# VectorE's order written out in the tiles of seven products: the fifth product's addition, S3's subtraction and S4's split

## The chip, the cores and the metric

The kernel runs on one core of one Trainium2 chip. The metric is the device time of one execution in microseconds (us); lower is better. A core has five engines that run their own instruction streams and wait for each other through semaphores: TensorE (PE in the profile, with its weight loads as PEld), VectorE (DVE), ScalarE (ACT), GpSimd (POOL) and SyncE (SP, which issues DMAs here).

## The reference

An attention layer is followed by two feed-forward layers. The change lies in the second of these (`_moe2_ref`), whose first half computes a gate and a value from the same input and multiplies them:

```python
def _moe2_ref(x, w_gate, w_val, w_out):       # x is 896 x 768, w_gate and w_val 768 x 1536
    g = x @ w_gate
    silu = g * (1.0 / (1.0 + np.exp(-g)))
    val = x @ w_val
    return (silu * val @ w_out).astype(np.float32)
```

All inputs arrive as float64 or float32 and the matmuls run on pairs of rounded float32 numbers: each operand is split into a high part (a rounding copy) and a low part (what the copy left out), and a product is high x high + high x low + low x high.

## The kernel before

The 1536 gate and value columns are worked off in 12 tiles `fc` of 128 columns. Tiles 1 to 6 (`ff2_gv_seven`) do not compute gate and value apart. They take the 128 gate columns and the 128 value columns of the tile as the rows of a 2 x 2 block matrix, whose columns are the two halves of the 768 inputs, and multiply it with the 2 x 2 blocks of x (two halves of the inputs, two halves of 448 tokens) in seven block products in place of eight (Winograd's form of Strassen's scheme). A block product is 9 matmuls of 448 columns (`product`: three 128-row pieces, three matmuls each).

The left factors are A11 and A12 (the gate's two halves), A22 (the value's second half) and four sums: S1 = value half 1 + value half 2, S3 = gate half 1 - value half 1, S2 = S1 - gate half 1, S4 = gate half 2 - S2. Their order on TensorE in tiles 2 to 6 is: A11 into bank `g`; S2 into bank `b`; A12, added into bank `g`; S3, added into bank `b`; S1 into bank `c` (the fifth); A22 into bank `e`; S4, added into bank `c`. Since the S4 product adds into bank `c`, it cannot start before VectorE has read the S1 product out of that bank.

What the other engines do in a tile, with the names that the trace shows:

- ScalarE copies bank `g` into `p1` (`ee<-g`) before the A12 product may add to that bank, and later takes Silu of it (a second `ee<-g`).
- VectorE adds products up in buffer `ee`: `u2 = p1 + b` (`ee<-ee,b`), `p1 = p1 + b` after the S3 product (`ee<-ee,b` again), `c22 = p1 + c` (the fifth product's addition, `ee<-ee,c`), `p1 = p1 + e` (`ee<-ee,e`), two multiplications into `s`, and `u2 = u2 + c` (the second `ee<-ee,c`). The tile's end is ScalarE's Silu of `u2` (`ee<-ee`), a multiplication on VectorE (`s<-ee`, 320 columns) and one on GpSimd (`ee<-ee`, 128 columns).
- The weights of the next tile are prepared meanwhile. Raw gate and value weights `wg_raw`, `wv_raw` are converted by two ScalarE instructions each (`wg<-wg_raw`, `wg<-wg`) and one VectorE instruction (`wg<-wg_raw,wg`). `sum_steps` returns the steps that make the sums and split them. GpSimd adds S1 (`t<-wv`) and subtracts S3 (`wv<-wg,wv`); VectorE subtracts S2 (`wg<-t,wg`) and S4 (`wg<-wg`); each split is a ScalarE copy and a VectorE subtraction: A11 and A12 together into `g_0` (`first`), S3 and S1 into `g_2` (`second`), S2 and S4 together into `g_1` or `g_3` by turns (`third`), A22 into `w` (`fourth`). The float32 gate weights of two tiles on share a buffer with those that `third` splits, so their conversion waits for that split.
- The results of the tile before are split for the second matrix product by `late()`: 384 columns (`a<-s`), a GpSimd subtraction of two result blocks (`s<-s,s`), and 128 columns (`a<-ee`).

ScalarE, TensorE and GpSimd run in the order in which the code is written (`pinned`); in tiles 2 to 6 the order on VectorE is set by the scheduler that builds the program. Every instruction waits for its place on its own engine.

Of the kernel before, what the change touches and what calls it, by code (L numbers as in the profile page):

```python
# [10 lines left out]
AF = mybir.ActivationFunctionType  # L11
# [26 lines left out]
class Kernel:  # L38
# [637 lines left out]
    def ff2_gv_first(self):  # L676

        V, n, mult, sub = self.V, self.HN, ALU.mult, ALU.subtract
        nc = self.nc
        sums, a, s2, s31, s24, a22 = self.sum_steps(1)  # L680
        sums()
        self.pinned = (nc.tensor, nc.vector, nc.scalar)
        ga = self.gv_product(0, 0, n, 0)
        self.x_hi(0)
        a[0]()
        a[1]()
        self.x_lo(0)
        self.x_hi(1)
        va = self.gv_product(0, 1, n, 0)
        sg, sb = self.sg  # L690
        self.A.activation(sg, ga, AF.Silu)
        s2()
        self.x_hi(2)
        s24[0]()
        V.tensor_tensor(sg, va, sg, op=mult)
        self.x_lo(1)
        s24[1]()
        gb = self.gv_product(0, 0, 512, n)
        self.x_hi(3)
        hi, lo = self.A11[0]  # L700
        self.hi_act(hi, sg)
        a22[0]()
        self.x_lo(2)
        self.lo_dve(lo, sg, hi)
        for f in s31:
            f()
        self.A.activation(sb, gb, AF.Silu)
        a22[1]()
        self.x_lo(3)
        vb = self.gv_product(0, 1, 512, n)  # L710
        steps = self.sum_steps(2)
        V.tensor_tensor(self.S1f[:, 0], vb[:, :n], sb[:, :n], op=mult)
        V.tensor_tensor(sb[:, n:], vb[:, n:], sb[:, n:], op=mult)
        V.tensor_tensor(self.S3f[:, 0], sg, self.S1f[:, 0], op=sub)
        self.split(self.A61[0], sb[:, n:])
        return steps

    def sum_steps(self, fc):

        add, sub = ALU.add, ALU.subtract  # L720
        if fc > self.KD + 1:
            return (lambda: None,) * 6
        f = []
        for n, w in zip("gv", (self.w_gate, self.w_val)):
            src = w[:, fc * 128:(fc + 1) * 128].rearrange("(k p) f -> p k f", p=128)
            f.append(self.f32_shifted(self.load_shifted(src, f"w{n}_{fc}"), f"w{n}_{fc}", (n == "v") * (1 + (fc > 2))))
        g, (v, rest) = f
        if fc > self.KD:
            d = [self.g4[m].rearrange("p (u x) -> p u x", u=2) for m in (2, 3)]

            def gate():
                self.split([d[0][:, u] for u in range(2)], g)

            def value():
                self.split([d[1][:, u] for u in range(2)], v)

            self.gvs[fc] = [t.rearrange("p u (k f) -> p u k f", f=128) for t in d]
            none = ()
            return rest, (value,), lambda: None, (gate,), none, none
        g, v = (t.rearrange("p (h x) -> p h x", h=2) for t in (g, v))  # L740
        s1 = self.t1
        pair = lambda t: [t.rearrange("p (h u x) -> p h u x", h=2, u=2)[:, :, u] for u in range(2)]
        t = self.gvs[fc] = [self.g4[0], self.g4[1 + fc % 2 * 2], self.g4[2], self.w1]
        S = self.G if fc > 1 else self.V

        def sums():
            rest()
            S.tensor_tensor(s1, v[:, 0], v[:, 1], op=add)
            S.tensor_tensor(v[:, 0], g[:, 0], v[:, 0], op=sub)

        def two(d, x):
            return lambda: self.hi_act(d[0], x), lambda: self.lo_dve(d[1], x, d[0])

        def s2():
            self.V.tensor_tensor(g[:, 0], s1, g[:, 0], op=sub)
            self.V.tensor_tensor(g[:, 1], g[:, 1], g[:, 0], op=sub)

        hi, lo = pair(t[2])
        s3, s1s = (two((hi[:, m], lo[:, m]), x) for m, x in enumerate((v[:, 0], s1)))
        return (sums, two(pair(t[0]), g), s2, s3[:1] + s1s[:1] + s3[1:] + s1s[1:], two(pair(t[1]), g),  # L760
                two([self.w1[:, u] for u in range(2)], v[:, 1]))

    def ff2_gv_seven(self, fc, steps):

        V, G, add, mult = self.V, self.G, ALU.add, ALU.mult
        n, k, ee = self.HN, fc % self.KD, self.ee
        a, s24, s31, a22 = self.gvs[fc]
        half = lambda t, h: t.rearrange("p (h u k f) -> p h u k f", h=2, u=2, k=3)[:, h]
        A11, A12, S2, S4, S3, S1 = (half(t, h) for t in (a, s24, s31) for h in range(2))
        A22 = a22.rearrange("p u (k f) -> p u k f", k=3)  # L770
        X = lambda kh, th: [[self.x2[3 * kh + c][:, u, 448 * th:448 * th + 448] for u in range(2)] for c in range(3)]
        T1, T2, T3, T4 = ([[t[:, u, c] for u in range(2)] for c in range(3)] for t in self.T)
        bank = lambda m: self.pt.tile([128, 512], F32, name=f"{m}_{fc}", tag="m")[:, :448]

        def product(acc, w, x, start):
            for c in range(3):
                self.mm3(acc, (w[:, 0, c], w[:, 1, c]), x[c], start and c == 0, c == 2, not start)

        sg, c22, p1, u2 = (ee[:, 448 * m:448 * m + 448] for m in range(4))
        last = fc == self.KD  # L780
        sums, first, s2, second, third, fourth = steps
        run = lambda fs: [f() for f in fs]
        a = bank("g")
        product(a, A11, X(0, 0), True)
        self.A.activation(p1, a, AF.Copy)
        sums()
        if fc > 1:
            self.late()
        if last:
            run(first)  # L790
        if fc == 1:
            d = bank("d")
            product(d, S4, X(1, 1), True)
            product(a, A12, X(1, 0), False)
        b = bank("b")
        product(b, S2, T2, True)
        V.tensor_tensor(u2, p1, b, op=add)
        if fc == 1:
            V.tensor_tensor(u2, u2, d, op=add)
            c = bank("c")  # L800
            product(c, S1, T1, True)
        else:
            product(a, A12, X(1, 0), False)
        if not last:
            run(first)
            s2()
            if fc == 1:
                self.A.activation(sg, a, AF.Silu)
                run(third)
        if fc > 1:  # L810
            self.A.activation(sg, a, AF.Silu)
        product(b, S3, T3, False)
        V.tensor_tensor(p1, p1, b, op=add)
        if fc > 1:
            c = bank("c")
            product(c, S1, T1, True)
        V.tensor_tensor(c22, p1, c, op=add)
        run(second)
        e = bank("e")
        product(e, A22, T4, True)  # L820
        V.tensor_tensor(p1, p1, e, op=add)
        if fc > 1:
            run(third)
        run(fourth)
        if fc > 1:
            product(c, S4, X(1, 1), False)
        V.tensor_tensor(u2, u2, c, op=add)
        if last:
            V.tensor_tensor(p1, p1, sg, op=mult)
            self.A.activation(u2, u2, AF.Silu)  # L830
            V.tensor_tensor(c22, c22, u2, op=mult)
            self.split(self.A12[k], p1[:, :n])
            V.tensor_tensor(self.S1f[:, k, :64], self.S1f[:, k, :64], p1[:, n:], op=add)
            V.tensor_tensor(self.S1f[:, k, 64:], self.S1f[:, k, 64:], c22[:, :320], op=add)
            for w, src in ((slice(0, 64), p1[:, n:]), (slice(64, 512), c22)):
                self.split([p[:, w] for p in self.A22[k]], src)
            return
        pinned = self.pinned
        if fc == 1:
            self.pinned += (self.nc.vector,)  # L840
        V.tensor_tensor(self.S3f[:, k], p1[:, :n], sg[:, :n], op=mult)
        V.tensor_tensor(self.S1f[:, k, :64], p1[:, n:], sg[:, n:], op=mult)
        steps = self.sum_steps(fc + 2)
        self.pinned = pinned
        self.A.activation(u2, u2, AF.Silu)
        V.tensor_tensor(self.S1f[:, k, 64:], c22[:, :320], u2[:, :320], op=mult)
        G.tensor_tensor(c22[:, 320:], c22[:, 320:], u2[:, 320:], op=mult)

        def late():
            self.split(self.A11[k], self.S3f[:, k])  # L850
            G.tensor_tensor(self.S3f[:, k], self.S3f[:, k], self.S1f[:, k], op=ALU.subtract)
            self.split(self.A61[k], c22[:, 320:])

        self.late = late
        return steps

    def split(self, d, src):

# [390 lines left out]
```

## Time and profile before

| what | value |
|---|---|
| median of three runs | 478.46 us (478.14 to 478.77) |
| profiled execution | 477.85 us, of which its span 476.1 us |
| TensorE busy | 469.9 us, 99% of the span |
| VectorE busy | 381.6 us, 80% |
| ScalarE busy | 306.4 us, 64% |
| GpSimd busy | 44.5 us, 9% |
| tiles 1 to 6 on TensorE | 241.53 to 322.10 us |
| granted TensorE clock | 0.999 of full speed |

Times in the trace count from the span's start. A row of the timeline gives the start, the duration, the engine, the instruction with what it writes and reads, and in brackets how long the engine had been idle and what ended that. TensorE being busy 99% of the span does not say that its matmuls run back to back: the record of a matmul spans its stay in the pipeline. What a stretch costs is read from the starts of successive products.

### The profile page before, as it was taken

The numbers are of one execution on the slowest core, as the hardware profiler recorded it, in microseconds if no ns is written. First come the engines' busy times: TensorE is split into PE (matmuls) and PEld (weight loads), VectorE is DVE, ScalarE is ACT, GpSimd is POOL, SyncE is SP. The second block draws the span as 40 slices with busy tenths as digits, with TensorE's granted clock in tenths as the row PEclk, the third lists the DMA queues.
The fourth block names the chain that finished last, engine by engine and source line by source line (L and its number), as shares of the span: only waits on it lengthen the run. The fifth ranks groups of instructions, "written<-read, shape, count | busy, mean of one in ns | idle before, by whom it ended". The sixth has DMA issues, their size and how long they took to land.

```text
span 476.1 us, 7684 instructions
## 1 busy us (share of the span) xinstructions
PE 469.9 (99%) x2988; PEld 386.1 (81%) x2988; DVE 381.6 (80%) x636; ACT 306.4 (64%) x445; POOL 44.5 (9%) x82
## 2 busy tenths in 40 slices
PE   9999999999999999999999999999999999999997
PEld 7445454538888899898989888889998899999996
DVE  3689999987779996765878899888666748999991
ACT  5999999941224798986857555688777736435220
POOL 1020101021000010000011333410000000000000
PEclk9999999999999999999999999999999999999999
DMA  6986565002000316255042234445666642010012
GB/s 186 214 204 143 136 185 148 21 2 89 0 1 5 126 47 200 89 184 172 19 132 67 83 118 132 133 132 185 213 199 199 200 131 66 1 67 2 18 60 89
DMA packets 65060, 52.33 MB, mean 110 GB/s; under 512 B 35584, under 2 KB 61952, under 8 KB 64256
## 3 DMA queue, kind: packets, MB, share of 16 engines
q1 hardware_dynamic: 64992, 51.85, 36.6%
q8 instruction: 23, 0.38, 0.3%
q14 instruction: 13, 0.11, 0.1%
q0 software_dynamic: 32, 0.00, 0.0%
HBM read 49.09 MB, written 2.75 MB: 109 GB/s over the span
## 4 chain that ended last, share of the span: by engine, by line
PE 90%; DVE 3%; ACT 3%; POOL 2%; issue 1%
PE p L30 16%; PE x L30 12%; PE h L30 12%; PE g L30 12%; PE v L30 9%; PE pv L30 8%; PE sc L30 7%; PE S L30 4%; PE b L30 2%; PE c L30 2%; PE lt L30 1%; ACT wg L30 1%; ACT wv L30 1%; POOL wv L30 1%; PE e L30 1%
## 5 line engine op out<-in xcount | busy, mean ns | idle before, releaser
L30 PE MATMUL g<-x,g 128*128 128x384 f32 (+2 forms) x324 | 69.9, 366 | 0.0
L30 PEld LDWEIGHTS g<-x,g 128*128 128x128 f32 x324 | 59.1, 188 | 7.5 <-ACT ee L30 1.5
L30 PE MATMUL h<-wi,x 128*128 128x512 f32 x252 | 59.1, 392 | 0.0
L30 PEld LDWEIGHTS h<-wi,x 128*128 128x128 f32 x252 | 46.8, 188 | 11.2 <-issue 1.5
L30 ACT ACTIVATE P<-sc,consts 112x896 f32<-112x896 f32 x48 | 45.4, 1010 | 3.7 <-PE sc L30 2.1
L30 PE MATMUL v<-x,g 128*128 128x384 f32 (+1 forms) x216 | 45.1, 362 | 0.0
L30 PEld LDWEIGHTS v<-x,g 128*128 128x128 f32 x216 | 39.1, 188 | 4.2
L30 ACT ACTIVATE P<-P,consts 112x3584 f32<-112x3584 f32 (+1 forms) x13 | 39.7, 3062 | 0.1
L30 PE MATMUL pv<-P,v 112*32 112x448 f32 x384 | 38.5, 540 | 0.0
L30 PEld LDWEIGHTS sc<-ks 64*112 64x112 f32 x288 | 23.3, 171 | 18.2 <-issue 7.7
L30 PE MATMUL sc<-ks 64*112 64x448 f32 x288 | 35.8, 378 | 0.3
L30 PE MATMUL x<-lB,wo 128*128 128x256 f32 (+1 forms) x192 | 35.2, 337 | 0.0
L30 PEld LDWEIGHTS x<-lB,wo 128*128 128x128 f32 x192 | 29.6, 189 | 3.4
L30 ACT ACTIVATE ee<-h,sms 128x512 f32<-128x512 f32 x14 | 9.5, 684 | 33.2 <-DVE sms L30 33.2
L30 PEld LDWEIGHTS pv<-P,v 112*32 112x32 f32 x384 | 12.2, 110 | 22.9 <-issue 20.2
L30 PE MATMUL x<-lA,wo 128*128 128x384 f32 x144 | 27.2, 338 | 0.0
L30 PE MATMUL p<-w,a 128*128 128x384 f32 x144 | 26.8, 334 | 0.0
L30 PEld LDWEIGHTS x<-lA,wo 128*128 128x128 f32 x144 | 25.2, 188 | 0.5
L30 PEld LDWEIGHTS p<-w,a 128*128 128x128 f32 x144 | 25.2, 188 | 0.1
L30 ACT ACTIVATE g<-wg 128x768 fp32r<-128x768 f32 x18 | 15.1, 840 | 14.8 <-DVE wg L30 12.8
L30 PE MATMUL b<-a,g 128*128 128x448 f32 x108 | 23.9, 366 | 0.0
L30 POOL COPY sm<-tr 32x14 f32<-32x14 f32 x48 | 15.0, 312 | 92.1 <-DVE tr L30 90.6
(214 smaller groups left out, 921.4 us busy)
## 6 DMA issues: line engine op xcount, KB each, us to landing
wg_raw<-in_moe_w_gate_dram SPq DMA_DIRECT2D x12, 765.8 KB, 4.2
wv_raw<-in_moe_w_val_dram SPq DMA_DIRECT2D x11, 765.8 KB, 4.3
wi_raw<-in_moe_w_in_dram SPq DMA_DIRECT2D x6, 1024.0 KB, 6.1
w_raw<-in_moe_w_out_dram SPq DMA_DIRECT2D x6, 767.6 KB, 4.3
wo_raw<-in_moe_w_out_dram SPq DMA_DIRECT2D x6, 512.0 KB, 3.4
wo_raw<-in_moe_w_out_dram SPq DMA_DIRECT2D x6, 510.5 KB, 3.5
v<-in_v_dram SPq DMA_DIRECT2D x24, 112.0 KB, 3.4
kq<-in_k_dram SPq DMA_DIRECT2D x22, 112.0 KB, 2.8
```

What stands on the lines that cost most here:

```text
L30: i = f(*a, **k)
```

## The change

In tiles 2 to 5 VectorE runs in the order of the code as well, in a branch of its own. In it the fifth product's addition stands ahead of S2's subtraction; S2's and S4's subtractions stand together, and then come the splits of S3, of S2 and S4, and of S1 (before, S1's copy stood ahead of that of S2 and S4 on ScalarE, and S4's split was the last of the three on VectorE). The subtraction of two result blocks in `late()` runs on VectorE and no longer on GpSimd; that holds for tiles 2 to 6. The tile's end became a function (`tail`).

```diff
--- before.py
+++ after.py
@@ -677,7 +677,7 @@
 
         V, n, mult, sub = self.V, self.HN, ALU.mult, ALU.subtract
         nc = self.nc
-        sums, a, s2, s31, s24, a22 = self.sum_steps(1)
+        sums, a, s2, s3, s1, s24, a22 = self.sum_steps(1)
         sums()
         self.pinned = (nc.tensor, nc.vector, nc.scalar)
         ga = self.gv_product(0, 0, n, 0)
@@ -702,7 +702,7 @@
         a22[0]()
         self.x_lo(2)
         self.lo_dve(lo, sg, hi)
-        for f in s31:
+        for f in s3[:1] + s1[:1] + s3[1:] + s1[1:]:
             f()
         self.A.activation(sb, gb, AF.Silu)
         a22[1]()
@@ -719,7 +719,7 @@
 
         add, sub = ALU.add, ALU.subtract
         if fc > self.KD + 1:
-            return (lambda: None,) * 6
+            return (lambda: None,) * 7
         f = []
         for n, w in zip("gv", (self.w_gate, self.w_val)):
             src = w[:, fc * 128:(fc + 1) * 128].rearrange("(k p) f -> p k f", p=128)
@@ -736,7 +736,7 @@
 
             self.gvs[fc] = [t.rearrange("p u (k f) -> p u k f", f=128) for t in d]
             none = ()
-            return rest, (value,), lambda: None, (gate,), none, none
+            return rest, (value,), lambda: None, (gate,), none, none, none
         g, v = (t.rearrange("p (h x) -> p h x", h=2) for t in (g, v))
         s1 = self.t1
         pair = lambda t: [t.rearrange("p (h u x) -> p h u x", h=2, u=2)[:, :, u] for u in range(2)]
@@ -757,7 +757,7 @@
 
         hi, lo = pair(t[2])
         s3, s1s = (two((hi[:, m], lo[:, m]), x) for m, x in enumerate((v[:, 0], s1)))
-        return (sums, two(pair(t[0]), g), s2, s3[:1] + s1s[:1] + s3[1:] + s1s[1:], two(pair(t[1]), g),
+        return (sums, two(pair(t[0]), g), s2, s3, s1s, two(pair(t[1]), g),
                 two([self.w1[:, u] for u in range(2)], v[:, 1]))
 
     def ff2_gv_seven(self, fc, steps):
@@ -778,10 +778,44 @@
 
         sg, c22, p1, u2 = (ee[:, 448 * m:448 * m + 448] for m in range(4))
         last = fc == self.KD
-        sums, first, s2, second, third, fourth = steps
+        sums, first, s2, s3, s1, third, fourth = steps
+        second = s3[:1] + s1[:1] + s3[1:] + s1[1:]
         run = lambda fs: [f() for f in fs]
         a = bank("g")
         product(a, A11, X(0, 0), True)
+        if 1 < fc and not last:
+            pinned = self.pinned
+            self.pinned += (self.nc.vector,)
+            self.A.activation(p1, a, AF.Copy)
+            b = bank("b")
+            product(b, S2, T2, True)
+            V.tensor_tensor(u2, p1, b, op=add)
+            sums()
+            self.late()
+            product(a, A12, X(1, 0), False)
+            run(first)
+            self.A.activation(sg, a, AF.Silu)
+            product(b, S3, T3, False)
+            V.tensor_tensor(p1, p1, b, op=add)
+            c = bank("c")
+            product(c, S1, T1, True)
+            V.tensor_tensor(c22, p1, c, op=add)
+            s2()
+            run(s3)
+            run(third)
+            run(s1)
+            e = bank("e")
+            product(e, A22, T4, True)
+            V.tensor_tensor(p1, p1, e, op=add)
+            V.tensor_tensor(self.S3f[:, k], p1[:, :n], sg[:, :n], op=mult)
+            V.tensor_tensor(self.S1f[:, k, :64], p1[:, n:], sg[:, n:], op=mult)
+            run(fourth)
+            product(c, S4, X(1, 1), False)
+            V.tensor_tensor(u2, u2, c, op=add)
+            steps = self.sum_steps(fc + 2)
+            self.tail(k, c22, u2)
+            self.pinned = pinned
+            return steps
         self.A.activation(p1, a, AF.Copy)
         sums()
         if fc > 1:
@@ -842,17 +876,22 @@
         V.tensor_tensor(self.S1f[:, k, :64], p1[:, n:], sg[:, n:], op=mult)
         steps = self.sum_steps(fc + 2)
         self.pinned = pinned
+        self.tail(k, c22, u2)
+        return steps
+
+    def tail(self, k, c22, u2):
+
+        V, G, mult = self.V, self.G, ALU.mult
         self.A.activation(u2, u2, AF.Silu)
         V.tensor_tensor(self.S1f[:, k, 64:], c22[:, :320], u2[:, :320], op=mult)
         G.tensor_tensor(c22[:, 320:], c22[:, 320:], u2[:, 320:], op=mult)
 
         def late():
             self.split(self.A11[k], self.S3f[:, k])
-            G.tensor_tensor(self.S3f[:, k], self.S3f[:, k], self.S1f[:, k], op=ALU.subtract)
+            V.tensor_tensor(self.S3f[:, k], self.S3f[:, k], self.S1f[:, k], op=ALU.subtract)
             self.split(self.A61[k], c22[:, 320:])
 
         self.late = late
-        return steps
 
     def split(self, d, src):
 
```

VectorE in tile 3, from the split of the previous tile's 384 result columns on (the numbers behind the names count buffers: `a_2484` results split, `g_0_1928` to `g_3_1931` weights split, `b`, `c`, `e` banks), before:

```order
L30 TENSOR_TENSOR a_2484<-s_2487,a_2484 128x384
L30 TENSOR_TENSOR a_2484<-ee,a_2484 128x128
L30 TENSOR_TENSOR g_0_1928<-wg_2826,g_0_1928 128x2x384
L30 TENSOR_TENSOR ee<-ee,b_2857 128x448
L30 TENSOR_TENSOR wg_2826<-t_2489,wg_2826 128x384
L30 TENSOR_TENSOR ee<-ee,c_2892 128x448
L30 TENSOR_TENSOR g_2_1930<-wv_2832,g_2_1930 128x384
L30 TENSOR_TENSOR wg_2826<-wg_2826 128x384
L30 TENSOR_TENSOR g_2_1930<-t_2489,g_2_1930 128x384
L30 TENSOR_TENSOR ee<-ee,e_2907 128x448
L30 TENSOR_TENSOR g_1_1929<-wg_2826,g_1_1929 128x2x384
L30 TENSOR_TENSOR s_2487<-ee 128x384
```

and now:

```order
L30 TENSOR_TENSOR a_2484<-s_2487,a_2484 128x384
L30 TENSOR_TENSOR s_2487<-s_2487,s_2486 128x384
L30 TENSOR_TENSOR a_2484<-ee,a_2484 128x128
L30 TENSOR_TENSOR g_0_1928<-wg_2826,g_0_1928 128x2x384
L30 TENSOR_TENSOR ee<-ee,b_2847 128x448
L30 TENSOR_TENSOR ee<-ee,c_2890 128x448
L30 TENSOR_TENSOR wg_2826<-t_2489,wg_2826 128x384
L30 TENSOR_TENSOR wg_2826<-wg_2826 128x384
L30 TENSOR_TENSOR g_2_1930<-wv_2832,g_2_1930 128x384
L30 TENSOR_TENSOR g_1_1929<-wg_2826,g_1_1929 128x2x384
L30 TENSOR_TENSOR g_2_1930<-t_2489,g_2_1930 128x384
L30 TENSOR_TENSOR ee<-ee,e_2909 128x448
```

The subtraction `s<-s,s` is new in the second place, the fifth product's addition has moved ahead of both `wg` subtractions, which stand together, and the split of `wg` into `g_1` has moved ahead of that of `t` into `g_2` and of the addition from bank `e`.

GpSimd at the end of tile 2's and tile 3's sums, as a piece of the difference (`t` is S1, `wv` takes S3, `ee` is the tile's end):

```order
 L30 TENSOR_TENSOR t_2489<-wv_2722 128x384
 L30 TENSOR_TENSOR wv_2722<-wg_2716,wv_2722 128x384
-L30 TENSOR_TENSOR s_2487<-s_2487,s_2486 128x384
 L30 TENSOR_TENSOR ee<-ee 128x128
 L30 TENSOR_TENSOR t_2489<-wv_2832 128x384
 L30 TENSOR_TENSOR wv_2832<-wg_2826,wv_2832 128x384
-L30 TENSOR_TENSOR s_2487<-s_2487,s_2486 128x384
 L30 TENSOR_TENSOR ee<-ee 128x128
```

Only the subtraction of the result blocks has gone; the two sums of each tile stand as they did.

ScalarE in tile 3, around the copies that split the sums, as a piece of the difference:

```order
 L30 ACTIVATE ee<-g_2836 128x448
 L30 ACTIVATE g_2_1930<-wv_2832 128x384
-L30 ACTIVATE g_2_1930<-t_2489 128x384
 L30 ACTIVATE g_1_1929<-wg_2826 128x2x384
+L30 ACTIVATE g_2_1930<-t_2489 128x384
 L30 ACTIVATE w_2488<-wv_2832 128x384
```

The copy of S2 and S4 (`g_1<-wg`) has moved ahead of that of S1 (`g_2<-t`). In the tiles 6 to 11 the scheduler's order of conversions and splits on VectorE and ScalarE also differs in places from the one before; TensorE's order is the same throughout.

## Rows read from the trace of the kernel before

**Rows 1.** The page's busy time by engine: us, share, instructions.

```profile
PE 469.9 (99%) x2988; PEld 386.1 (81%) x2988; DVE 381.6 (80%) x636; ACT 306.4 (64%) x445; POOL 44.5 (9%) x82
```

**Rows 2.** Waits of weight loads by releaser: us in total, times, longest.

```profile
PEld c L30 <- DVE ee L30: 3.2, 4, 0.8
...
PEld g L30 <- ACT ee L30: 1.5, 5, 0.4
```

**Rows 3.** Timeline of TensorE: starts of products in tiles 1 to 6.

```profile
241.53 1.99 PE L30 MATMUL g<-x,g 128*128 128x448 f32 x9
...
254.29 1.99 PE L30 MATMUL g<-x,g 128*128 128x448 f32 x9
...
277.35 2.02 PE L30 MATMUL e<-a,w 128*128 128x448 f32 x9
279.69 2.09 PE L30 MATMUL c<-x,g 128*128 128x448 f32 x9 [0.32 <-DVE ee L30]
...
309.08 1.99 PE L30 MATMUL g<-x,g 128*128 128x448 f32 x9
```

**Rows 4.** Timeline of VectorE, tile 3 into tile 4.

```profile
273.51 0.96 DVE L30 SCALAR_TENSOR_TENSOR wv<-wv_raw,wv 128x768 uint32<-128x768 uint32 x1 [0.39 <-ACT wv L30]
274.39 0.55 DVE L30 TENSOR_TENSOR a<-s,a 128x384 fp32r<-128x384 f32 x1
274.86 1.11 DVE L30 TENSOR_TENSOR a<-ee,a 128x128 fp32r<-128x128 f32 x1
275.89 0.94 DVE L30 TENSOR_TENSOR g<-wg,g 128x768 fp32r<-128x768 f32 x1
276.76 0.61 DVE L30 TENSOR_TENSOR ee<-ee,b 128x448 f32<-128x448 f32 x1
277.75 1.35 DVE L30 TENSOR_TENSOR wg<-t,wg 128x384 f32<-128x384 f32 x1 [0.38 <-POOL wv L30]
279.03 0.61 DVE L30 TENSOR_TENSOR ee<-ee,c 128x448 f32<-128x448 f32 x1
...
281.50 0.95 DVE L30 TENSOR_TENSOR g<-wg,g 128x768 fp32r<-128x768 f32 x1
282.37 0.69 DVE L30 TENSOR_TENSOR s<-ee 128x384 f32<-128x384 f32 x2
...
283.44 0.61 DVE L30 TENSOR_TENSOR ee<-ee,c 128x448 f32<-128x448 f32 x1
...
287.25 0.96 DVE L30 SCALAR_TENSOR_TENSOR wv<-wv_raw,wv 128x768 uint32<-128x768 uint32 x1 [0.38 <-ACT wv L30]
```

**Rows 5.** Timeline of ScalarE, end of tile 3.

```profile
280.61 0.85 ACT L30 ACTIVATE g<-wg 128x768 fp32r<-128x768 f32 x1 [1.92 <-DVE wg L30]
...
282.48 1.01 ACT L30 ACTIVATE wg<-wg_raw,consts 128x768 f32<-128x768 int8 x1 [0.61 <-DVE g L30]
...
284.37 0.56 ACT L30 ACTIVATE ee<-ee 128x448 f32<-128x448 f32 x1
284.83 0.53 ACT L30 ACTIVATE ee<-g 128x448 f32<-128x448 f32 x1
```

**Rows 6.** Timeline of GpSimd, tile 3.

```profile
271.25 0.77 POOL L30 TENSOR_TENSOR ee<-ee 128x128 f32<-128x128 f32 x1 [6.30 <-ACT ee L30]
274.55 1.27 POOL L30 TENSOR_TENSOR t<-wv 128x384 f32<-128x384 f32 x1 [2.52 <-DVE wv L30]
275.90 1.82 POOL L30 TENSOR_TENSOR wv<-wg,wv 128x384 f32<-128x384 f32 x1
277.67 1.02 POOL L30 TENSOR_TENSOR s<-s,s 128x384 f32<-128x384 f32 x1
```

**Rows 7.** Timeline of VectorE, end of tile 2 and start of tile 3.

```profile
270.74 0.96 DVE L30 SCALAR_TENSOR_TENSOR wg<-wg_raw,wg 128x768 uint32<-128x768 uint32 x1 [0.43 <-ACT wg L30]
271.62 0.75 DVE L30 TENSOR_TENSOR s<-ee 128x320 f32<-128x320 f32 x1
272.50 0.62 DVE L30 TENSOR_TENSOR ee<-ee,b 128x448 f32<-128x448 f32 x1
```

## Prediction

> **What bounds the kernel now.** I read the busy shares first, then the waits of TensorE's weight loads, then the starts of its products, and then, for one tile, VectorE, ScalarE and GpSimd row by row. The busy shares put TensorE at 99% [rows 1], so at first sight nothing off TensorE can matter. The product starts say otherwise. Tile 1 runs without a wait, from 241.53 to 254.29: seven products in 12.76 us, 1.82 each. Tiles 2 to 5 take from 254.29 to 309.08, which is 54.79 us or 13.70 a tile, 3.75 us in all above four unhindered tiles [rows 3]. The waits give two places: the S4 product (written `c<-x,g`) waits for VectorE's `ee`, 0.8 us at most and once in each of the four tiles; and the A12 product (a `g` bank) waits for ScalarE's copy, up to 0.4 us [rows 2]. In tile 3 the A22 product starts at 277.35 and S4's at 279.69, 2.34 us later instead of 1.82 [rows 3].
>
> The reader should not stop at that wait. Follow tile 3 on VectorE and see what each row stands behind. The value weights' conversion starts at 273.51; the splits of `s`, of 128 columns and of `g_0` follow (274.39, 274.86, 275.89), the addition from bank `b` at 276.76, S2's subtraction at 277.75 (0.38 us idle before it, for GpSimd's S3), the fifth product's addition at 279.03, and in the end S2 and S4's split, 281.50 to 282.45 [rows 4]. For that split waits ScalarE's conversion of the gate weights of two tiles on, at 282.48 (it stood idle 0.61 us for it); then come Silu of `u2` at 284.37, the copy of bank `g` at 284.83, and two conversions [rows 5], whose result VectorE takes up at 287.25 [rows 4]. That closes a circle: 287.25 - 273.51 = 13.74 us, 8.94 on VectorE (273.51 to 282.45) and 4.80 on ScalarE. TensorE is not in it. Its 13.70 a tile is the circle's period, and its two waits are where the circle shows. Within the circle Silu to the next conversion takes 287.25 - 284.37 = 2.88. The last addition of a tile, `u2 + c`, ends at 283.44 + 0.61 = 284.05, which is 0.32 before the Silu that needs it [rows 4, 5]: a second circle through that addition has 0.32 us to spare.
>
> **The change, part by part.** I lay tile 3 out anew from the same 273.51. An instruction of VectorE starts 0.08 before its predecessor's end where nothing holds it (273.51 + 0.96 = 274.47, next at 274.39) [rows 4], and a semaphore between engines costs 0.03 (282.45 to 282.48) [rows 4, 5].
>
> First the subtraction that moves. It is 384 columns, 0.55 us where nothing blocks it, like the split at 274.39 [rows 4]. But it comes at about 274.98, while GpSimd's S1 sum, issued at 274.55, is at work until 274.55 + 1.27 = 275.82 [rows 6]. Before, the 128-column split stood there: 1.11 us, to 275.97, 0.15 after GpSimd's end [rows 4]. S2's subtraction met GpSimd's `s<-s,s` in the same way: that ended at 277.67 + 1.02 = 278.69, and the subtraction 0.41 later, at 279.10 [rows 4, 6]. So a VectorE instruction with both inputs in SBUF waits for a GpSimd instruction that came first. The reverse holds too: GpSimd's S3 was issued at 275.90, behind the split at 275.89, and ended at 277.72, 0.89 after that split's end at 276.83 [rows 4, 6]. The addition from a bank at 276.76 took its usual 0.61 beside it [rows 4].
>
> What happens with GpSimd waiting and VectorE's instructions back to back? GpSimd's multiplication came at 271.25 inside the conversion 270.74 to 271.70, and the next VectorE row, at 271.62, took 0.75 and ended 0.35 after GpSimd's end at 272.02 [rows 6, 7]. The one that waited went first. Hence, in the new order:
>
> - the subtraction ends 0.41 after S1's sum: 276.23;
> - S3's sum, waiting since 275.90, goes next and ends at 276.23 + 0.89 = 277.12;
> - the 128-column split, issued at 276.15, ends 0.15 later at 277.27, where it ended at 275.97 before;
> - `g_0`'s split 277.19 to 278.13, the addition from `b` to 278.66.
>
> The Trainium skill (SBUF — State Buffer, section "Who interferes with whom") states that a VectorE instruction with two SBUF inputs contends with a GpSimd instruction that reads SBUF, and that the one issued first holds the shared ports for its whole length. This trace agrees (1.11 us for the 128-column split). By that rule the period below is 14.36 us; by the opposite, that VectorE's next instruction keeps the ports, it is the 13.52 us of the second rival.
>
> Then the new neighbours. The fifth addition now reads what the addition before it wrote, S4's subtraction what S2's wrote, and the multiplications what the addition from `e` wrote. Such a wait on one's own engine may cost nothing (0.08 before the end) or 0.13 (272.37 to 272.50, where other engines were waited for as well) [rows 7]; I take 0.04 after the end, near the middle. Fifth addition 278.70 to 279.31; S2's subtraction to 279.78, without the 0.80 us of being blocked, since `s<-s,s` is gone from GpSimd, and without the 0.38 of waiting; S4's subtraction 279.82 to 280.37; S3's split 280.29 to 280.84. Here VectorE stands idle: ScalarE's copy takes 0.85 [rows 5], 280.40 to 281.25, and only then comes S2 and S4's split, 281.28 to 282.23. Before, S1's split and the addition from `e` filled that time.
>
> So the first circle closes: 282.23 against 282.45, a gain of 0.22. But S1's split (0.55), the addition from `e` (0.61), the multiplications (0.69), the value's split (0.55) and `u2 + c` (0.61) now all stand behind it: they end at 282.70, 283.23, 283.96, 284.43 and 284.96. Before, `u2 + c` ended at 284.05 [rows 4]; the 0.32 to spare is used up, and Silu of `u2` comes at 284.99 instead of 284.37. With 2.88 to the next conversion the period is 284.99 + 2.88 - 273.51 = 14.36 us, 0.62 above 13.74. ScalarE's earlier conversions buy nothing, since they now wait in front of the Silu.
>
> The fifth addition's own gain is real and covered: TensorE's S4 product starts at about 279.36 in place of 279.69. Three products of 1.82 later, at 284.8, it comes to the next A12 product, but the copy ahead of that starts 0.46 after the Silu (284.83 - 284.37) and takes 0.53 [rows 5]: it ends at 284.99 + 0.99 = 285.98, so TensorE waits there for some 1.1 us, where the weight load waited 0.3 on average [rows 2]. The circle passes from tile 2 to 3, 3 to 4, 4 to 5 and 5 to 6: 4 x 0.62 = 2.48 us. From tile 6's A12 product on TensorE had no wait for these, so the lateness stays to the end. In tile 6 GpSimd has no sums to block the subtraction, and its 0.55 us lie under the products. The sum against the profiled execution is 477.85 + 2.48 = 480.33; the median of the runs stands 0.61 above the profiled execution, so 480.94 us.
>
> Bounds: the three waits on one's own engine move the period by 3 x 0.12 down or 3 x 0.09 up, which is -1.4 or +1.1 us over four tiles: 479.5 to 482.0.
>
> **The rivals.** First, faster: the moved subtraction is not blocked, nor the split behind it. The place is 274.98, the price 1.54 us a tile: 274.98 + 0.55 = 275.53, and the 128-column split, 0.28 us by the slope between 384 and 768 columns (0.55 and 0.95) [rows 4], would end at 275.73 and not at 277.27; then the last addition ends at 283.42, the period is 12.82, hardly above TensorE's own 12.76, and the kernel gains 4 x 0.92 = 3.7 us: 474.8. For it speaks that TensorE's wait for the fifth addition would then be gone; against it, three rows where the one that came later stood still [rows 4, 6, 7]. It decides from 0.86 us of the 1.54 on: there the period is 13.50, 4 x 0.24 below today's.
>
> Second, about the same: the subtraction waits for S1's sum, but the 128-column split slips in ahead of S3's. Then everything from there on is 0.84 earlier (276.43 against 277.27), the last addition ends at 284.12, the period is 13.52, and four tiles give -0.9 us: 477.6. For it speaks that S3's sum lost once, by 0.01 us [rows 4, 6]; against it, that in that row VectorE was issued first, and here it is issued 0.25 later.
>
> Third, slower still: in tiles 7 to 11 the new order puts conversions of the next matrix, about 1 us each like the one at 282.48 [rows 5], ahead of the splits of gate and value weights. One product waiting once for such a split would cost up to 1 us, two 2: about 482 to 483.
>
> **How the numbers follow.** My forecast has 0.70, the third rival 0.06, the second 0.14, the first 0.10. The prediction is 480.9 us, the likeliest case. The range goes down to the second rival's 477.6 and up to the upper bound with the runs' spread of 0.3, 482.3; outside lie the first rival and part of the third. About 0.2%, 0.96 us, is what a measurement here can tell from no change. Slower by more: 0.70 + 0.06 less 0.02 for the lowest bound together, 0.74. Within: 0.10 of the second rival and that 0.02. Faster: the first rival and 0.04 of the second, 0.14.
>
> **What would show it.** In the new profile, in tiles 3 to 5: the period between value conversions near 14.4; the subtraction `s<-s,s` on VectorE lasting about 1.25 us with S1's sum beside it; the 128-column split above 1.0 us beside S3's sum; S2's subtraction back at 0.55; about 0.5 us idle ahead of the split of S2 and S4, ended by ScalarE; ScalarE's Silu of `u2` waiting for VectorE's `ee`; and the larger TensorE wait at the A12 product. A subtraction of 0.55 us would make the prediction wrong at its first step; a 128-column split of 0.3 us at its second; a Silu of `u2` that starts right behind ScalarE's conversions would say that the second circle does not bind.

## The result and the profile after

The changed kernel takes 481.66 us (median of four runs, 481.07 to 481.85) beside 478.30 for the kernel before (with a fourth run; the three known when the prediction was made gave 478.46): a ratio of 1.0069, 95% interval 1.0051 to 1.0086. It is slower by 3.4 us; the prediction was 480.9, in a range from 477.6 to 482.3. The profiled execution has a span of 479.9 us where the one before had 476.1.

On the names: the "S3's subtraction" of the title is the subtraction of two result blocks, which the code calls `S3f` and `S1f` and the trace `s<-s,s`. The weights' sum S3 (`wv<-wg,wv`) stays on GpSimd.

TensorE first: its products at the places that matter, in tiles 1 to 7 (the rows of before are [rows 3]).

```profile
242.40 1.99 PE L30 MATMUL g<-x,g 128*128 128x448 f32 x9
...
255.16 1.99 PE L30 MATMUL g<-x,g 128*128 128x448 f32 x9
...
278.83 1.99 PE L30 MATMUL e<-a,w 128*128 128x448 f32 x9
281.02 2.09 PE L30 MATMUL c<-x,g 128*128 128x448 f32 x9 [0.20 <-DVE ee L30]
...
284.78 1.98 PE L30 MATMUL b<-a,g 128*128 128x448 f32 x9
287.73 2.09 PE L30 MATMUL g<-x,g 128*128 128x448 f32 x9 [0.96 <-ACT ee L30]
...
311.88 1.98 PE L30 MATMUL g<-x,g 128*128 128x448 f32 x9
...
325.89 3.31 PE L30 MATMUL g<-x,g 128*128 128x384 f32 x18
```

The A22 product starts at 278.83 and S4's at 281.02: 2.19 us, where before it was 2.34. The wait for the fifth addition has become smaller, not gone. The large wait is now elsewhere: S2's product starts at 284.78 and A12's at 287.73, 2.95 us, where before it was 1.97 (283.44 to 285.41) and an unhindered product takes 1.82, and ScalarE's copy ends the wait. Tiles 2 to 5 take from 255.16 to 311.88, 56.72 us in place of 54.79 [rows 3]; with the wait in front of tile 6's A12 product the tiles 1 to 6 take 325.89 - 242.40 = 83.49 us. Before they ran from 241.53 to 322.10, 80.57 us. From there to the end of the span it is 154.0 us in both. The 0.87 us by which tile 1 starts later lies ahead of everything that the change touches; in the profiles of this study that start lies between 241.16 and 243.53.

The waits of the weight loads, summed by who ended them (before: [rows 2]):

```profile
PEld g L30 <- ACT ee L30: 5.5, 5, 1.3
...
PEld c L30 <- DVE ee L30: 2.3, 4, 0.6
```

The `c` waits fell from 3.2 to 2.3 us, the `g` waits rose from 1.5 to 5.5.

VectorE in tile 3, from the value weights' conversion to the next tile's (before: [rows 4]):

```profile
275.10 0.96 DVE L30 SCALAR_TENSOR_TENSOR wv<-wv_raw,wv 128x768 uint32<-128x768 uint32 x1 [0.65 <-ACT wv L30]
...
276.56 1.26 DVE L30 TENSOR_TENSOR s<-s,s 128x384 f32<-128x384 f32 x1
277.74 1.10 DVE L30 TENSOR_TENSOR a<-ee,a 128x128 fp32r<-128x128 f32 x1
...
279.63 0.61 DVE L30 TENSOR_TENSOR ee<-ee,b 128x448 f32<-128x448 f32 x1
280.35 0.62 DVE L30 TENSOR_TENSOR ee<-ee,c 128x448 f32<-128x448 f32 x1
280.89 0.55 DVE L30 TENSOR_TENSOR wg<-t,wg 128x384 f32<-128x384 f32 x1
...
282.94 0.96 DVE L30 TENSOR_TENSOR g<-wg,g 128x768 fp32r<-128x768 f32 x1 [0.44 <-ACT g L30]
...
284.29 0.61 DVE L30 TENSOR_TENSOR ee<-ee,e 128x448 f32<-128x448 f32 x1
284.94 0.69 DVE L30 TENSOR_TENSOR s<-ee 128x384 f32<-128x384 f32 x2
...
286.01 0.61 DVE L30 TENSOR_TENSOR ee<-ee,c 128x448 f32<-128x448 f32 x1
...
289.56 0.96 DVE L30 SCALAR_TENSOR_TENSOR wv<-wv_raw,wv 128x768 uint32<-128x768 uint32 x1 [0.65 <-ACT wv L30]
```

The circle now takes 289.56 - 275.10 = 14.46 us, where it took 13.74. The subtraction `s<-s,s` lasts 1.26 us and the split behind it 1.10; S2's subtraction is back at 0.55. Ahead of S2 and S4's split (282.94) VectorE stands idle 0.44 us, ended by ScalarE, and that split ends 8.80 us after 275.10; but `u2 + c` (286.01) ends at 286.62. What ScalarE does with that:

```profile
283.94 1.00 ACT L30 ACTIVATE wg<-wg_raw,consts 128x768 f32<-128x768 int8 x1 [0.20 <-DVE g L30]
...
286.66 0.58 ACT L30 ACTIVATE ee<-ee 128x448 f32<-128x448 f32 x1 [0.76 <-DVE ee L30]
```

ScalarE's conversions begin 0.20 us after it fell idle, but it then stands 0.76 us in front of the Silu of `u2`, for VectorE's `ee`. Before it went straight from the conversions to the Silu [rows 5]. GpSimd in the same tile (before: [rows 6]):

```profile
276.14 1.26 POOL L30 TENSOR_TENSOR t<-wv 128x384 f32<-128x384 f32 x1 [2.79 <-DVE wv L30]
277.48 1.22 POOL L30 TENSOR_TENSOR wv<-wg,wv 128x384 f32<-128x384 f32 x1
```

S1's sum ends at 277.40; the subtraction ends 0.42 us later, S3's sum at 278.70, the split of 128 columns at 278.84.

### The profile page after: what moved, and what is told of

Same layout as the page of the kernel before. It is cut to its first block, busy times and chain, and to the rows that moved or that the text cites. A ratio compares the mean times of both kernels' runs of the same rounds, so it can differ in the third digit from the quotient of the medians.

```text
span 479.9 us, 7672 instructions
## 1 busy us (share of the span) xinstructions
PE 470.8 (98%) x2988; PEld 386.7 (81%) x2988; DVE 382.3 (80%) x641; ACT 307.0 (64%) x445; POOL 36.0 (8%) x77
## 4 chain that ended last, share of the span: by engine, by line
PE 85%; DVE 9%; ACT 3%; issue 2%; DVEq 0%; ACTq 0%
PE p L30 16%; PE x L30 12%; PE h L30 12%; PE g L30 10%; PE v L30 9%; PE pv L30 8%; PE sc L30 7%; PE S L30 4%; DVE ee L30 2%; DVE g L30 2%; ACT wv L30 2%; DVE a L30 1%; PE lt L30 1%; DVE wg L30 1%; PE T L30 1%
## 5 line engine op out<-in xcount | busy, mean ns | idle before, releaser
L30 PE MATMUL S<-P,ones 112*32 112x448 f32 x192 | 22.4, 549 | 0.0
```

Of the source, the lines that this page charges most:

```text
L30: i = f(*a, **k)
```

## The experiments

Theory: the tiles run at the period of the longer of two circles through VectorE and ScalarE, one through S2 and S4's split, one through the tile's last addition; TensorE's waits only follow. Rivals: the cost is VectorE's added and blocked work; TensorE's wait for the fifth addition is what can be won; the order of the tiles behind costs. In every kernel below VectorE's order in tiles 2 to 5 is written out; `s2.parts` are S2's and S4's subtractions. The diffs are against the changed kernel, and the period is the time from one value conversion to the next, as above (before 13.74, changed 14.46). The kernel before measured 478.44 us beside the first four experiments and 478.25 beside the last three.

**The subtraction alone.**

```diff
+            s2.parts[0]()
             V.tensor_tensor(c22, p1, c, op=add)
-            s2()
-            run(s3)
-            run(third)
-            run(s1)
+            s3[0]()
+            s1[0]()
+            s3[1]()
+            s2.parts[1]()
+            s1[1]()
             e = bank("e")
             product(e, A22, T4, True)
             V.tensor_tensor(p1, p1, e, op=add)
+            run(third)
```

> Only the result blocks' subtraction moves to VectorE; the fifth addition and S4's split stay where they were before. Theory of the two circles: the subtraction and the split behind it push everything 1.3 us later, but S2's subtraction is then neither blocked (0.80 us) nor waiting for GpSimd (0.38 us), so S2 and S4's split ends where it did; period 13.8 us against 13.74, the kernel within 0.5 us of before (478 to 479). Rival, that VectorE's added and blocked work is the cost: about 2.9 us slower than before, as the whole change (481). A second rival, that the changed order in the tiles 6 to 11 costs, gives a loss behind tile 6, and this kernel has that order.

Measured: 478.49 us beside 478.44, ratio 1.000 (0.999 to 1.0011). VectorE in its tile 3:

```profile
273.15 0.96 DVE L30 SCALAR_TENSOR_TENSOR wv<-wv_raw,wv 128x768 uint32<-128x768 uint32 x1 [0.37 <-ACT wv L30]
...
274.61 1.26 DVE L30 TENSOR_TENSOR s<-s,s 128x384 f32<-128x384 f32 x1
275.79 1.10 DVE L30 TENSOR_TENSOR a<-ee,a 128x128 fp32r<-128x128 f32 x1
...
278.21 0.55 DVE L30 TENSOR_TENSOR wg<-t,wg 128x384 f32<-128x384 f32 x1
...
286.91 0.96 DVE L30 SCALAR_TENSOR_TENSOR wv<-wv_raw,wv 128x768 uint32<-128x768 uint32 x1 [0.38 <-ACT wv L30]
```

The period is 13.76. The subtraction is blocked for as long as in the changed kernel (1.26, and 1.10 for the split), yet S2's subtraction, which follows at once and unblocked, ends at 278.76, 5.61 us after the conversion, where before it was 279.10 - 273.51 = 5.59 [rows 4]. So in this order VectorE's added and blocked work costs nothing on balance, since S2's subtraction loses its own blocking and waiting in exchange; in the changed order it does cost something, as the sixth experiment shows. The changed order in the tiles behind, which this kernel shares with the changed one, costs nothing. Both rivals fall as the whole of the cost.

**S4's split alone.**

```diff
+            s2.parts[0]()
             V.tensor_tensor(c22, p1, c, op=add)
-            s2()
-            run(s3)
+            s3[0]()
+            s3[1]()
+            s2.parts[1]()
             run(third)
             run(s1)
...
-            V.tensor_tensor(self.S3f[:, k], self.S3f[:, k], self.S1f[:, k], op=ALU.subtract)
+            G.tensor_tensor(self.S3f[:, k], self.S3f[:, k], self.S1f[:, k], op=ALU.subtract)
```

> Only the split of S2 and S4 (with S4's subtraction ahead of it) stands ahead of that of S1, on ScalarE and VectorE; the subtraction stays on GpSimd and the fifth addition behind S2's subtraction. Theory of the two circles: VectorE idles about 0.45 us for ScalarE's copy, and S1's split and the addition from bank e go behind, so the last addition comes about 1.1 us later and Silu of u2 closes the longer circle; period 14.5 to 14.6 us, 0.8 above before, 3 to 3.5 us slower (481.5 to 482). Rival, that the subtraction on VectorE is the cost: no change, 478.3.

Measured: 481.68 us, ratio 1.0071 (1.0053 to 1.0088). VectorE in its tile 3:

```profile
274.55 0.96 DVE L30 SCALAR_TENSOR_TENSOR wv<-wv_raw,wv 128x768 uint32<-128x768 uint32 x1 [0.66 <-ACT wv L30]
...
281.05 0.55 DVE L30 TENSOR_TENSOR wg<-wg 128x384 f32<-128x384 f32 x1
282.51 0.96 DVE L30 TENSOR_TENSOR g<-wg,g 128x768 fp32r<-128x768 f32 x1 [0.91 <-ACT g L30]
...
285.58 0.61 DVE L30 TENSOR_TENSOR ee<-ee,c 128x448 f32<-128x448 f32 x1
...
289.13 0.96 DVE L30 SCALAR_TENSOR_TENSOR wv<-wv_raw,wv 128x768 uint32<-128x768 uint32 x1 [0.66 <-ACT wv L30]
```

The period is 14.58. VectorE idles 0.91 us ahead of the split, for ScalarE's copy; S1's split and the addition from `e` follow it, and `u2 + c` ends at 286.19, 2.72 us behind the split's end at 283.47, where it was 1.60 before (284.05 - 282.45 [rows 4]). This one move is as costly as the whole change. The waits of the weight loads on `c` are as before:

```profile
PEld c L30 <- DVE ee L30: 3.3, 4, 0.8
```

One thing differs from the change: here S4's subtraction (281.05) stands directly ahead of its split, behind S3's split; in the change it stands ahead of S3's split, which then fills 0.47 us of the time for ScalarE's copy.

**The fifth product's addition alone.**

```diff
             V.tensor_tensor(c22, p1, c, op=add)
-            s2()
-            run(s3)
-            run(third)
-            run(s1)
+            s2.parts[0]()
+            s3[0]()
+            s1[0]()
+            s3[1]()
+            s2.parts[1]()
+            s1[1]()
             e = bank("e")
             product(e, A22, T4, True)
             V.tensor_tensor(p1, p1, e, op=add)
+            run(third)
...
-            V.tensor_tensor(self.S3f[:, k], self.S3f[:, k], self.S1f[:, k], op=ALU.subtract)
+            G.tensor_tensor(self.S3f[:, k], self.S3f[:, k], self.S1f[:, k], op=ALU.subtract)
```

> Only the fifth product's addition stands ahead of S2's subtraction; the subtraction stays on GpSimd and S4's split where it was. Theory of the two circles: the addition falls into the time in which S2's subtraction waits for GpSimd anyway, so all behind it comes 0.54 us earlier; period 13.2 us, 2.2 us faster than before (476.1). Rival, that TensorE's wait for the fifth addition is the whole cost: that wait goes (0.6 to 0.7 us a tile) and the kernel gains 2.8 us (475.5); rival, that it only moves: no change.

Measured: 475.88 us, ratio 0.9954 (0.9941 to 0.9968), 2.6 us faster than the kernel before. VectorE in its tile 3:

```profile
273.12 0.96 DVE L30 SCALAR_TENSOR_TENSOR wv<-wv_raw,wv 128x768 uint32<-128x768 uint32 x1 [0.39 <-ACT wv L30]
...
277.07 0.62 DVE L30 TENSOR_TENSOR ee<-ee,c 128x448 f32<-128x448 f32 x1
277.61 1.09 DVE L30 TENSOR_TENSOR wg<-t,wg 128x384 f32<-128x384 f32 x1
...
286.31 0.96 DVE L30 SCALAR_TENSOR_TENSOR wv<-wv_raw,wv 128x768 uint32<-128x768 uint32 x1 [0.38 <-ACT wv L30]
```

The addition (277.07) stands in the time in which S2's subtraction waited before; S2's is still blocked by GpSimd (1.09 us), but ends at 278.70, 5.58 us after the conversion, just as before, with the addition already done. The period is 13.19, 0.55 less, as the theory had it. The waits of weight loads on `c` are gone from the list, as the rival had it too; those on `g` are left, 2.1 us in all. The rival's 475.5 is too near in time to fall by it; the seventh experiment separates the two.

**The whole change without S4's split.** The diff is the third experiment's without its last two lines, so the subtraction stays on VectorE.

> The whole change but S4's split, which stays behind S1's split and the addition from bank e, as before. Theory of the two circles: the last addition follows S2 and S4's split within 1.6 us again, so the first circle binds: period 13.8 to 13.9 us, 0.1 to 0.7 us slower than before (478.4 to 479). Rival, that the subtraction on VectorE is the cost: as slow as the whole change (481.7).

Measured: 479.09 us, ratio 1.0018 (1.0007 to 1.0029). The value conversion in its tiles 3 and 4:

```profile
273.72 0.96 DVE L30 SCALAR_TENSOR_TENSOR wv<-wv_raw,wv 128x768 uint32<-128x768 uint32 x1 [0.38 <-ACT wv L30]
...
287.66 0.96 DVE L30 SCALAR_TENSOR_TENSOR wv<-wv_raw,wv 128x768 uint32<-128x768 uint32 x1 [0.38 <-ACT wv L30]
```

The period is 13.94, a little above the 13.8 to 13.9 expected; the rival's 481.7 falls. Beside the first experiment the fifth addition now stands ahead of S2's subtraction, and that brings nothing, it costs 0.18 us: with `s<-s,s` gone from GpSimd there is no waiting left for it to fill, and it now follows the addition whose result it reads, starting 0.10 us behind that one's end where VectorE otherwise starts 0.08 ahead of it. What makes 13.94 into 14.46 is the move of S4's split, with S4's subtraction going ahead of S3's split.

**The last addition early.**

```diff
             V.tensor_tensor(p1, p1, e, op=add)
+            product(c, S4, X(1, 1), False)
+            V.tensor_tensor(u2, u2, c, op=add)
             V.tensor_tensor(self.S3f[:, k], p1[:, :n], sg[:, :n], op=mult)
             V.tensor_tensor(self.S1f[:, k, :64], p1[:, n:], sg[:, n:], op=mult)
             run(fourth)
-            product(c, S4, X(1, 1), False)
-            V.tensor_tensor(u2, u2, c, op=add)
```

> The whole change, but the last addition of a tile (u2 + c) stands ahead of the multiplications and of the value's split, behind the addition from bank e. Nothing is taken away. Theory of the two circles: the circle through the last addition gets about 1.1 us shorter, and both now take 13.5 to 13.7 us where the whole change takes 14.46; 478 us, like before or slightly faster. Rival, that the moved subtraction's and the splits' blocking is what costs: nothing is blocked less here, so it stays at 481.7.

Measured: 478.58 us, ratio to before 1.0008 (0.9998 to 1.0017). VectorE around the end of its tile 3:

```profile
275.53 0.96 DVE L30 SCALAR_TENSOR_TENSOR wv<-wv_raw,wv 128x768 uint32<-128x768 uint32 x1
...
285.25 0.62 DVE L30 TENSOR_TENSOR ee<-ee,c 128x448 f32<-128x448 f32 x1
...
289.14 0.95 DVE L30 SCALAR_TENSOR_TENSOR wv<-wv_raw,wv 128x768 uint32<-128x768 uint32 x1
```

The same instructions, none blocked less, and the period falls from 14.46 to 13.61 us. So it is the second circle, through the last addition, that bound the changed kernel: leaving that addition where it was due wins the whole loss back, with all the blocking still there. VectorE now goes from one instruction to the next without a wait at the conversion (289.14). S2 and S4's split ends 8.80 us after the conversion, as in the changed kernel, and 4.81 us later the next conversion starts, so the first circle sets the pace now. The four passes from tile 2 to tile 6 sum to 54.58 us in this profile, 0.37 less than before, yet the medians lie 0.33 us the other way; where that comes from is open.

**The subtraction in the gap.**

```diff
-            run(third)
+            third[0]()
+            self.subtract()
+            third[1]()
             run(s1)
...
-            V.tensor_tensor(self.S3f[:, k], self.S3f[:, k], self.S1f[:, k], op=ALU.subtract)
+            self.subtract = lambda: V.tensor_tensor(self.S3f[:, k], self.S3f[:, k], self.S1f[:, k], op=ALU.subtract)
+            if k == self.KD - 1:
+                self.subtract()
```

> The whole change, but in tiles 2 to 5 the subtraction of the result blocks stands between S3's split and that of S2 and S4, where VectorE idles 0.44 us for ScalarE's copy and GpSimd is at rest. Theory: it takes 0.55 us there and is not blocked, the split of 128 columns waits for S1's sum as before, S3's sum goes behind the split of g_0; the period falls from 14.46 to 13.1 to 13.3 us, about 2 to 2.6 us faster than before (475.8 to 476.5). Rival, that the place of S4's split alone decides: 481.7 or little less, as the second experiment.

Measured: 476.28 us, ratio 0.9957 (0.9940 to 0.9973). VectorE in its tile 3:

```profile
273.71 0.96 DVE L30 SCALAR_TENSOR_TENSOR wv<-wv_raw,wv 128x768 uint32<-128x768 uint32 x1 [0.65 <-ACT wv L30]
...
279.73 0.55 DVE L30 TENSOR_TENSOR s<-s,s 128x384 f32<-128x384 f32 x1
280.26 0.96 DVE L30 TENSOR_TENSOR g<-wg,g 128x768 fp32r<-128x768 f32 x1
...
286.88 0.96 DVE L30 SCALAR_TENSOR_TENSOR wv<-wv_raw,wv 128x768 uint32<-128x768 uint32 x1 [0.65 <-ACT wv L30]
```

The subtraction takes 0.55 us where GpSimd rests, and the split behind it starts with no idle time; the period is 13.17. So with S4's split ahead the place of the subtraction is worth 1.29 us a tile, and that split's idle time was room for it. ScalarE still stands 0.76 us in front of the Silu of `u2`: the second circle binds here too, and it is shorter because everything on VectorE ahead of `u2 + c` comes 1.29 us sooner. The loss of the change can thus be won back on that circle from either side, by the addition's place or by the blocked work. The rival's 481.7 falls. By itself, in the first experiment, the same blocked subtraction had cost nothing, since the blocking and waiting of S2's subtraction went in exchange.

**The fifth addition early and the subtraction late.** S4's split is where it was, and GpSimd keeps the subtraction, one tile later, behind the multiplication at the tile's end. The order of the other steps is the third experiment's.

```diff
         G.tensor_tensor(c22[:, 320:], c22[:, 320:], u2[:, 320:], op=mult)
+        if k > 1:
+            self.subtract()
...
-            V.tensor_tensor(self.S3f[:, k], self.S3f[:, k], self.S1f[:, k], op=ALU.subtract)
+            self.subtract = lambda: G.tensor_tensor(self.S3f[:, k], self.S3f[:, k], self.S1f[:, k], op=ALU.subtract)
+            if k == self.KD - 1:
+                self.subtract()
```

> The fifth addition ahead of S2's subtraction, as in the third experiment, S4's split where it was, and the subtraction of the result blocks on GpSimd but one tile later, behind the multiplication at the tile's end, where GpSimd rests and VectorE adds from a bank. Theory: nothing blocks S2's subtraction any more, both circles (12.65 and 12.4 us) are shorter than TensorE's own 12.76 us, so TensorE becomes the bound in tiles 2 to 5; a period of 12.8 to 12.9, 3.4 to 3.8 us faster than before (474.6 to 475.0). Rival, that TensorE's wait for the fifth addition was all that could be had: as the third experiment, 475.9.

Measured: 474.23 us, ratio 0.9919 (0.9904 to 0.9934): 4.0 us faster than before, and 7.4 below the change's median. That is a little better than the 474.6 to 475.0 expected. The waits of weight loads, and GpSimd and VectorE in tile 3:

```profile
PEld g L30 <- ACT ee L30: 0.2, 1, 0.2
```

```profile
271.05 1.26 POOL L30 TENSOR_TENSOR s<-s,s 128x384 f32<-128x384 f32 x1
...
274.94 1.81 POOL L30 TENSOR_TENSOR wv<-wg,wv 128x384 f32<-128x384 f32 x1
```

```profile
271.57 0.62 DVE L30 TENSOR_TENSOR ee<-ee,b 128x448 f32<-128x448 f32 x1
272.56 0.96 DVE L30 SCALAR_TENSOR_TENSOR wv<-wv_raw,wv 128x768 uint32<-128x768 uint32 x1 [0.37 <-ACT wv L30]
...
274.94 0.95 DVE L30 TENSOR_TENSOR g<-wg,g 128x768 fp32r<-128x768 f32 x1
...
276.61 0.62 DVE L30 TENSOR_TENSOR ee<-ee,c 128x448 f32<-128x448 f32 x1 [0.19 <-PE c L30]
277.14 0.55 DVE L30 TENSOR_TENSOR wg<-t,wg 128x384 f32<-128x384 f32 x1
...
285.31 0.96 DVE L30 SCALAR_TENSOR_TENSOR wv<-wv_raw,wv 128x768 uint32<-128x768 uint32 x1 [0.38 <-ACT wv L30]
```

TensorE's waits in these tiles are down to 0.2 us, once. GpSimd's subtraction runs from 271.05 to 272.31, about half of it while VectorE adds from a bank (271.57 to 272.19) at its usual 0.62, and S2's subtraction is unblocked at 0.55. The period is 12.75 us, TensorE's own. The rival's 475.9 falls: what stood in the way in the third experiment was again the first circle, through S2's blocked subtraction, not a wait of TensorE.

## Why the prediction was right

By its own steps, with times from the value conversion's start, in tile 3 of the changed kernel (at 275.10):

| step | predicted | measured |
|---|---|---|
| subtraction ends | 2.72 | 2.72 |
| S3's sum ends | 3.61 | 3.60 |
| split of 128 columns ends | 3.76 | 3.74 |
| fifth addition ends | 5.80 | 5.87 |
| S2 and S4's split ends | 8.72 | 8.80 |
| `u2 + c` ends | 11.45 | 11.52 |
| Silu to the next conversion | 2.88 | 2.90 |
| period | 14.36 | 14.46 |

- **The bound.** TensorE was 99% busy and still not what set the tiles' pace: its wait for the fifth addition grew smaller in the changed kernel and the time grew; in the second experiment the `c` waits were as before (3.3 us beside 3.2) and the time grew as much.
- **The blocked subtraction and split.** Right, in all four tiles. The rule of the Trainium skill that was weighed there (SBUF — State Buffer, "Who interferes with whom") held there: 1.26 and 1.10 us in place of 0.55 and 0.28. The first and second rival fall with that. That the waiting GpSimd instruction goes first had been taken from one row, and the last section has a case in another kernel where it did not.
- **The waits on one's own engine.** 0.04 us was taken for each of three; they measured 0.11 (fifth addition), 0.03 (S4's subtraction, from 281.44 to 281.47) and 0.04 (multiplications). The 0.07 of the first is most of the 0.10 by which the period was taken too short. Over the four passes from tile 2 to tile 6 the loss is 2.9 us, where 2.48 was forecast.
- **The second circle.** Right, and shown twice: moving the last addition of the changed kernel takes 0.85 us off the period, and moving S4's split in the order of before adds 0.84.
- **The third rival.** From tile 6's end the span is 154.0 us in both; the first experiment has the same order there and costs nothing.
- **The total.** The medians lie 3.36 us apart, where 2.48 was forecast. The period's 0.10 a pass is 0.4 of the difference; the circle as measured gives 2.9, and the remaining 0.5 us is within the interval of the ratio (2.4 to 4.1 us) and is not traced to any place.

The parts do not add up: alone they measure +0.02, +0.84 and -0.55 us a tile, +0.31 together, while the change has +0.72. The fifth addition gains only while S2's subtraction waits for GpSimd, and the moved subtraction takes that wait away. S4's split loses less in the change (0.52 beside the fourth experiment) than alone; VectorE idles 0.44 us for the copy and not 0.91, because S4's subtraction stands further ahead.

## What to carry to other kernels

Where a busy engine shows short waits at one place in each pass, compare the length of the pass with the engine's own work, and follow what it waits for back through the other engines until it closes a circle; the circle's length is the pace, and a shorter visible wait helps only where the circle gets shorter too: the `c` waits shrank in the changed kernel, which was slower, and went in the third experiment, which was faster. Before an instruction is moved ahead of others, look at what those others lead to: here the split ended 0.14 us earlier in its own circle (8.80 us after the conversion in place of 8.94), and the last addition 0.98 later in the next (11.52 in place of 10.54). Work of VectorE and GpSimd that blocks the other belongs where the other engine rests or reads a bank: putting 1 us of GpSimd's work there, one tile later, took the third experiment's 475.88 to 474.23, and moving it to VectorE instead gave 479.09.

## What the runs showed of the hardware that was not expected

That a waiting GpSimd instruction goes ahead of VectorE's next one was forecast; not expected was how exactly it repeats, and that it fails once. In tiles 2 to 5 of the changed kernel the subtraction took 1.25 to 1.26 us and the split behind it 1.10 to 1.11. The one exception in tiles 2 to 6 of these nine profiles is the GpSimd multiplication at the end of tile 2 in the fifth experiment:

```profile
273.12 1.65 POOL L30 TENSOR_TENSOR ee<-ee 128x128 f32<-128x128 f32 x1 [7.75 <-ACT ee L30]
```

```profile
273.96 0.49 DVE L30 TENSOR_TENSOR s<-ee 128x320 f32<-128x320 f32 x1
```

It was issued inside VectorE's conversion (273.09 to 274.05), yet VectorE's next instruction went first, unblocked at 0.49 us, and GpSimd ended 0.32 behind it. In tiles 3 to 5 the same two instructions, as close to the conversion's start, took 1.24 to 1.25 and 0.76: there GpSimd went first. Why it differs is open. Where both are issued in the same hundredth, at 274.94 in the last experiment, VectorE's 0.95 us split went first and GpSimd's sum took 1.81.

And an addition that reads what the VectorE instruction before it wrote started 0.11 us after that one's end, about three times as late as the other two dependent pairs (0.03 and 0.04). It is the one of the three that also reads a product's bank, but that product was long done: it starts at 277.00 and the next one at 278.83, the addition at 280.35. Why it is later was not tried.
